# Attention scores in two visits a batch instead of five, with halves of 288 tokens, in a fused attention and mixture-of-experts kernel

## The chip, the cores and the metric

The kernel runs on one core of a Trainium2 chip, in one launch. The metric is the device time in microseconds (us) of that launch. Before the change the median of three timed runs is 524.84 us (524.31 to 526.43).

## The reference

Attention over 8 batches, 8 heads, 576 tokens and 64 values a head, with keys and values averaged over groups of 8 tokens (72 pooled keys); then a mixture of experts with 4 groups of 4 experts, one expert a token, on the 4608 x 512 result.

```
k_p = k.reshape(B, H, Sp, pool, D).mean(axis=3); v_p likewise     # pool = 8, Sp = 72
scores = scale * np.matmul(q, k_p.transpose(0, 1, 3, 2))
attn = np.exp(scores - scores.max(-1)); attn = attn / (attn.sum(-1) + 1e-09)
x = np.matmul(attn, v_p)              # -> (4608, 512) after joining the heads
g_idx = argmax(x @ w_group); g_w = softmax(x @ w_group)[g_idx]
e_idx = argmax(x @ w_expert[g_idx]);  e_w = softmax(...)[e_idx]
h = np.maximum(x @ w1[g, e], 0.0)     # 512 -> 1024
out = g_w * e_w * (h @ w2[g, e])      # 1024 -> 512
```

## The kernel before, in words

The work goes batch by batch (`b` = 0 to 7, 576 tokens each). While the experts' products of batch `b` run (class `Moe`, `m`), the attention of batch `b + 1` (`n`) is done between them, and the first steps of batch `b + 2` (`x`). Nearly all tokens of a batch choose one expert; its weights are loaded, and tokens with another expert are done behind the last batch (class `Left`).

The order is written out by hand in five plans, START, FIRST, SECOND, STEADY and LAST (lines 34 to 77): words such as `n.sc:1` or `m.up:3:0` are called one after the other by `run` (L880). START, FIRST and SECOND (batches 0 and 1) fix the order on all five engines. STEADY serves b = 2 to 6 and LAST b = 7; there the order is fixed on PE, DVE, POOL and SP, and ACT's is chosen by a scheduler. Every engine runs its instructions in its order.

The steps that matter here:

- `kr` (L252) folds 8 keys into one on DVE; `kt` (L282) transposes the pooled keys on PE into two `tp` banks: four transposes of 128 x 128 and, for the last 64 rows, one that reads partitions 64 to 127 alone (L286). ACT copies the result to `kT`. `qb` (L305) transposes the queries of a chunk on DVE into `qT`.
- `sc` (L310) is a **score visit**: the tokens of a batch lie in five chunks, `CH` (four of 128, one of 64), and one visit does a chunk. For each block of 32 tokens it issues 8 matmuls of 64 rows x 32 columns on parts of the PE array, into the two `sc` banks of PSUM. There is one pair of them (`ps_s`, L160), which the attention product `av` uses too.
- The softmax of a visit: `mx` (maximum, DVE, L329), `sb` (subtract on DVE, exponential on ACT, L335), `su_` (sum and reciprocal, DVE, L342), `nm` (scaling, POOL, L350), `pt` (transpose, DVE, L355).
- `av` (L363) multiplies the probabilities with the values for 256 or 320 tokens (`HALF`, L27), into the `sc` banks and two of the three `tp` banks. ACT takes the result, `avd` (L380) the low part on DVE. `rt` (L384), `route` and `main_expert` (L441) choose the experts; the count on PE (L437) is followed by the vote and by the weight loads on SP (L525).
- `load`, `cast` and `lo` bring a quarter of a weight matrix: DMA into one of 4 `sw` tiles, high part on ACT (L531), low part on POOL (L537). `split` is the last two.
- `up` (L543) does one of 8 blocks of 128 hidden values for one half: 12 matmuls over 256 or 320 tokens into one of three `mm` banks, then a ReLU on ACT (L556); `upd` (L558) takes the low part on DVE, and then the bank is free. `down` (L569) does a third of a chunk with 8 matmuls over 512 columns; after the third, ACT scales and stores. The last chunk of 64 tokens is L597 and is taken out by a copy on ACT (L602) and an add on DVE (L603).

One steady batch issues on PE: `up` of all blocks with four score visits between them, `av` twice, `rt` twice, 14 `down` with the routing, the key transposes and one score visit (the first of the batch after) between them.

Of the kernel before, what the change touches and what calls it, by code (L numbers as in the profile page):

```python
# [26 lines left out]
HALF = ((0, 256), (256, 320))  # L27
# [10 lines left out]
a.av:0:256 a.mx:2 a.sb:2 a.avd:0:256  # L38
# [20 lines left out]
m.load:2:3 m.up:1:1 m.upd:1:1 n.sc:2 n.mx:2 n.sb:2 n.qb:3 n.pt:1 x.load_k x.load_v
m.up:2:0 m.upd:2:0 n.su_:2 n.nm:2:p m.split:2:0 m.up:2:1 m.upd:2:1 m.up:3:0 m.upd:3:0 n.sc:3  # L60
n.mx:3 n.sb:3 n.qb:4 n.pt:2 m.up:3:1 m.upd:3:1 n.su_:3 n.nm:3:p m.split:2:1 m.up:4:0 m.upd:4:0 m.up:4:1 m.upd:4:1
n.sc:4 n.mx:4 n.sb:4 n.pt:3 m.up:5:0 m.upd:5:0 n.su_:4 n.nm:4:p m.split:2:2 m.up:5:1 m.upd:5:1 x.load_qb:0 x.load_qb:1
x.load_qb:2 x.load_qb:3 m.up:6:0 m.upd:6:0 m.split:2:3 m.up:7:0 m.upd:7:0 n.pt:4 n.av:0:256 n.avd:0:256 m.up:6:1 m.upd:6:1
m.up:7:1 m.upd:7:1 n.av:256:320 n.rt:0:256 n.avd:256:320
m.down:0 n.rt:256:320 x.kr:0 m.down:1 x.kr:1 m.down:2 n.route m.down:3 m.down:4 m.down:5 n.main_expert w.load:1:0 w.load:1:1 w.load:1:2 w.load:1:3
x.qb:0 n.gates n.gm_ n.keep_x m.down:6 x.vr:0 x.kt m.down:7 w.split:1:0 w.load:2:0 m.down:8 m.down:9
x.sc:0 x.mx:0 x.sb:0 x.qb:1 m.down:10 w.split:1:1 w.load:2:1 x.vr:1 x.vm m.down:11 x.su_:0 x.nm:0:p m.down:12 m.down:13
# [13 lines left out]
def attn_moe(ctx: ExitStack, tc: tile.TileContext, q, k, v, wg, we, w1, w2, out):  # L81
# [35 lines left out]
    probs = [keep.tile([128, 4, 160], F32, name=f"p{i}") for i in range(2)]  # L117
    for t in probs:
        nc.gpsimd.memset(t, 0.0)
    sums = [keep.tile([128, 4, 2, 2], F32, name=f"s{i}") for i in range(2)]  # L120
    for t in sums:
        nc.vector.memset(t, 1e-9)
# [57 lines left out]
    class Att:  # L180


        def __init__(s, b):
            s.b = b
            s.lt = s.v6 = s.pT = s.q = s.k = s.v = s.vf = None
            s.xt, s.qT, s.ss, s.su, s.ta, s.m = {}, {}, {}, {}, {}, {}

# [94 lines left out]
        def kt(s):  # L282
# [6 lines left out]
            nc.scalar.mul(out=s.kT[:, 512:576], in_=ps[1][:, 0:64], mul=0.015625)  # L289

        def qt(s, c):
# [10 lines left out]
            s.qT[c] = sm.tile([128, NG, 128], F32, name="qT")  # L302
            nc.scalar.copy(out=s.qT[c][:, :, 0:n], in_=ps.rearrange("p (g r) -> p g r", g=NG)[:, :, 0:n])

        def qb(s, c):  # L305
            o, n = CH[c]
            s.qT[c] = sm.tile([128, NG, 128], F32, name="qT")
            nc.vector.transpose(out=s.qT[c][:, :, 0:n], in_=s.q[:, 0:NG * S].rearrange("p (g t) -> p g t", g=NG)[:, :, o:o + n])

        def sc(s, c, where="s"):  # L310
            if where == "s":
                ps = ps_s.tile([128, 2, 512], F32, name="sc")
                s.ss[c] = [(slice(0, 2), ps)]
                ps = [ps[:, 0], ps[:, 1]]
            else:
                ps = [ps_m.tile([128, 512], F32, name="mm") for i in range(2)]
                s.ss[c] = [(slice(x, x + 1), ps[x].unsqueeze(1)) for x in range(2)]
            w = CH[c][1] // 32
            for t in range(w):
                for g in range(NG):  # L320
                    for x in range(2):
                        nc.tensor.matmul(ps[x][32 * g:32 * g + 32, SP * t:SP * t + SP], lhsT=s.qT[c][64 * x:64 * x + 64, g, 32 * t:32 * t + 32],  # L322
                                         rhs=s.kT[64 * x:64 * x + 64, SP * (2 * g + x):SP * (2 * g + x) + SP], start=(t == 0), stop=(t == w - 1))

        def views(s, c):
            w = CH[c][1] // 32
            return w, probs[(s.b * NC + c) % 2][:, 0:w, 0:2 * SP]

        def mx(s, c):  # L329
            w, p = s.views(c)  # L330
            m = s.m[c] = sm.tile([128, 2, 4], F32, name="mx")
            for x, ps in s.ss[c]:
                red(out=m[:, x, 0:w], in_=ps[:, :, 0:SP * w].rearrange("p x (t s) -> p x t s", s=SP), axis=AX.X, op=ALU.max)  # L333
# [594 lines left out]
```

## Time and profile before

| what | us |
|---|---|
| median of three timed runs | 524.84 |
| the profiled execution | 525.55 |
| its span, first to last instruction | 523.8 |
| PE busy in the span | 508.7 (97%) |
| DVE, POOL, ACT busy | 338.6, 257.1, 207.3 |

The profile is one execution. PE is TensorE with the matmuls, DVE VectorE, ACT ScalarE, POOL GpSimd, SP the queue that issues most DMAs. A row of a timeline merges equal instructions that follow one another: start, duration until the last has ended, engine, line, operation, `out<-in`, shape, count, and in brackets the idle time before it and what ended it. Matmuls overlap, so a row lasts a little beyond the start of the next; how long a stretch takes on PE is the distance between starts.

[...]

### The profile page before, as it was taken

Reading aid. Unit: us, or ns where it says so; the run is one execution under the profiler, and the core shown is the slowest. Engines: PE = TensorE matmul, PEld = TensorE weight load, DVE = VectorE, ACT = ScalarE, POOL = GpSimd, SP = SyncE. Lnnn points to the kernel's source line nnn. Section 1 sums busy time; section 2 is a strip of 40 time slices with the busy share of each in tenths; the row PEclk is TensorE's granted clock in tenths of the full one; section 3 lists DMA queues with packets and bytes.
Section 4 is the critical chain, followed back from the end, with each engine's and each line's share of the span. In section 5 each row is a group of like instructions: output and inputs, shape, how many; then the busy total and the mean of one; then the engine's idle time right before and its main releaser. Section 6 shows DMA issues by size and latency. Waiting matters only on the chain.

```text
span 523.8 us, 15045 instructions
## 1 busy us (share of the span) xinstructions
PE 508.7 (97%) x6061; PEld 446.4 (85%) x6061; DVE 338.6 (65%) x999; ACT 207.3 (40%) x394; POOL 257.1 (49%) x246
## 2 busy tenths in 40 slices
PE   8899989999989999999999999999999999999994
PEld 7698867898779988899889988899889988899873
DVE  6887878688366865397645956387646854287602
ACT  2444343453226531545235542455234541443211
POOL 2394866465536632867057741857049660511400
PEclk9999999999999999999999999999999999999998
DMA  8699398494256862749364771967555100835731
GB/s 284 182 261 197 85 257 229 73 241 103 52 173 181 236 99 79 244 148 186 73 199 155 211 119 45 332 229 201 91 169 185 63 1 21 268 125 195 231 139 36
DMA packets 118128, 83.75 MB, mean 160 GB/s; under 512 B 71034, under 2 KB 93818, under 8 KB 117800
## 3 DMA queue, kind: packets, MB, share of 16 engines
q1 hardware_dynamic: 113424, 75.70, 53.6%
q10 hardware_dynamic: 4600, 7.02, 3.8%
q8 instruction: 49, 0.80, 0.7%
q14 instruction: 23, 0.19, 0.1%
q0 software_dynamic: 32, 0.04, 0.0%
HBM read 77.31 MB, written 28.53 MB: 202 GB/s over the span
## 4 chain that ended last, share of the span: by engine, by line
PE 89%; DMA 4%; DVE 3%; POOL 1%; SPq 1%; issue 1%; ACT 1%; DVEq 0%; POOLq 0%
PE mm L554 34%; PE mm L580 32%; PE mm L597 5%; PE sc L322 5%; PE sc L373 4%; PE tp L390 3%; DMA vv<-in_v_dram 3%; DMA pT<-in_k_dram 1%; PE tp L285 1%; POOL vv L262 1%; PE tp L414 1%; PE tp L785 0%; PE tp L373 0%; PE tp L301 0%; PE tp L470 0%
## 5 line engine op out<-in xcount | busy, mean ns | idle before, releaser
L580 PE MATMUL mm<-w,ht 128*128 128x512 f32 x768 | 177.3, 383 | 0.0
L537 POOL TENSOR_TENSOR w<-sw,w 128x1024 fp32r<-128x1024 f32 (+2 forms) x87 | 148.7, 1731 | 40.3 <-ACT w L531 40.3
L580 PEld LDWEIGHTS mm<-w,ht 128*128 128x128 f32 x768 | 141.4, 189 | 21.6 <-issue 1.6
L554 PE MATMUL mm<-xb,w 128*128 128x320 f32 x768 | 115.9, 303 | 0.0
L554 PEld LDWEIGHTS mm<-xb,w 128*128 128x128 f32 x768 | 105.9, 189 | 4.3 <-issue 2.3
L554 PE MATMUL mm<-xa,w 128*128 128x256 f32 x768 | 96.3, 278 | 0.5 <-ACT xa L378 0.5
L554 PEld LDWEIGHTS mm<-xa,w 128*128 128x128 f32 x768 | 91.2, 191 | 3.5 <-ACT xa L378 1.0
L556 ACT ACTIVATE ht<-mm 128x320 fp32r<-128x320 f32 (+1 forms) x128 | 52.0, 408 | 81.3 <-PE mm L554 81.2
L353 POOL TENSOR_TENSOR p<-p,su 128x576 f32<-128x576 f32 (+1 forms) x40 | 42.2, 1057 | 71.5 <-DVE su L348 63.4
L531 ACT CAST w<-sw 128x1024 fp32r<-128x1024 f32 x64 | 66.0, 1041 | 20.5 <-DMA sw<-in_moe_w_dram 20.5
L566 DVE SCALAR_TENSOR_TENSOR ht<-mm,ht 128x160 fp32r<-128x160 f32 (+2 forms) x192 | 38.9, 258 | 18.2 <-ACT ht L556 17.7
L340 ACT ACTIVATE p<-p 128x576 f32<-128x576 f32 (+1 forms) x40 | 25.5, 637 | 54.5 <-DVE p L338 50.5
L491 POOL TENSOR_TENSOR mp<-oh,moh 128x80 f32<-128x80 f32 x8 | 3.4, 426 | 87.8 <-DVE moh L456 87.7
L591 ACT ACTIVATE y<-mm,gm 128x512 f32<-128x512 f32 x31 | 21.3, 686 | 52.3 <-PE mm L580 52.3
L333 DVE TENSOR_REDUCE mx<-sc 128x8 f32<-128x576 f32 (+1 forms) x38 | 26.1, 688 | 21.6 <-PE sc L322 21.6
L562 DVE SCALAR_TENSOR_TENSOR ht<-mm,ht 128x256 fp32r<-128x256 f32 x64 | 25.9, 406 | 14.3 <-ACT ht L556 14.0
L360 DVE STREAM_TRANSPOSE pT<-p 128x640 f32<-128x640 f32 (+1 forms) x40 | 30.5, 762 | 5.7 <-POOL p L353 5.7
L322 PE MATMUL sc<-kT,qT 64*32 64x72 f32 x2176 | 30.6, 229 | 2.0 <-DVE xa L382 1.6
L322 PEld LDWEIGHTS sc<-kT,qT 64*32 64x32 f32 x2176 | 23.9, 105 | 9.6 <-issue 7.0
L597 PE MATMUL mm<-w,ht 128*128 128x512 f32 x128 | 29.4, 381 | 0.0
L346 DVE TENSOR_REDUCE s<-p 128x8 f32<-128x576 f32 (+1 forms) x40 | 27.1, 677 | 1.2 <-ACT p L340 1.0
L338 DVE TENSOR_TENSOR p<-sc,mx 128x576 f32<-128x576 f32 (+1 forms) x38 | 26.4, 694 | 1.4
(212 smaller groups left out, 529.6 us busy)
## 6 DMA issues: line engine op xcount, KB each, us to landing
sw<-in_moe_w_dram SPq DMA_DIRECT2D x72, 512.0 KB
xscr<-xb SPq DMA_DIRECT2D x8, 1280.0 KB
vv<-in_v_dram SPq DMA_DIRECT2D x27, 320.0 KB
xscr<-xa SPq DMA_DIRECT2D x8, 1024.0 KB
q<-in_q_dram SPq DMA_DIRECT2D x112, 72.0 KB
kv<-in_k_dram SPq DMA_DIRECT2D x14, 512.0 KB
out_dram<-y ACTq DMA_DIRECT2D x23, 256.0 KB
pT<-xscr SPq DMA_DIRECT2D x4, 1152.0 KB
```

What stands on the lines that cost most here:

```text
L322: nc.tensor.matmul(ps[x][32 * g:32 * g + 32, SP * t:SP * t + SP], lhsT=s.qT[c][64 * x:64 * x + 64, g, 32 * t:32 * t + 32], rhs=s.kT[64 * x ...
L338: tt(out=p.rearrange("p t (x s) -> p x t s", x=2)[:, x], in0=ps[:, :, 0:SP * w].rearrange("p x (t s) -> p x t s", s=SP), in1=bc(s.m[c][:, ...
L346: red(out=two[:, :, :, 0], in_=p.rearrange("p t (x s) -> p t x s", x=2), axis=AX.X, op=ALU.add)
L353: (nc.vector if eng == "v" else nc.gpsimd).tensor_tensor(out=p, in0=p, in1=bc(s.su[c][:, 0:w], SP), op=ALU.mult)
L360: nc.vector.transpose(out=s.pT[:, :, o:o + n].rearrange("p j (t i) -> p t j i", i=32), in_=probs[(s.b * NC + c) % 2][:, 0:n // 32].rearran ...
L531: nc.scalar.copy(out=s.w[m, j][0], in_=raw)
L537: (nc.vector if eng == "v" else nc.gpsimd).tensor_tensor(out=wl[:, i:i + n], in0=s.raw[m, j][:, i:i + n], in1=wh[:, i:i + n].bitcast(F32), ...
L554: nc.tensor.matmul(ps[:, 0:n], lhsT=l[:, kc, fs], rhs=apart(s.a.xt[o][:, r, kc]), start=(kc == 0 and i == 0), stop=(kc == 3 and i == 2))
L556: nc.scalar.activation(out=halves(ht[:, sl]), in_=joined(ps[:, 0:n]), func=AF.Relu)
L566: stt(out=ht[:, at:at + hi - lo], in0=ps[:, a, lo:hi], scalar=0.0, in1=ht[:, t + lo:t + hi].bitcast(F32), op0=ALU.max, op1=ALU.subtract)
L580: nc.tensor.matmul(ps, lhsT=s.ht[f][:, 640 * l + o:640 * l + o + 128], rhs=apart(s.w[2, f // 2][r][:, f % 2, :]), start=(i == 0), stop=(i ...
L597: nc.tensor.matmul(ps, lhsT=s.ht[f][:, 512:640], rhs=apart(s.w[2, f // 2][r][:, f % 2, :]), start=(i == 0), stop=(i == 15))
```

## The change

From batch 3 on (`EARLY = 3`) the halves of attention and `up` are 288 and 288 tokens, and a half is also the chunk of a score visit: nine blocks of 32 tokens, two visits a batch. Seven blocks lie in the two `sc` banks, and two in two `tp` banks. The first visit's softmax goes in one step, the second's in a step A of four blocks and a step B of five. The exponential goes in pieces of at most five blocks. `probs` and `sums` become one tile each, `qT` one of 288 tokens. The key transposes take all 128 rows, for all batches. Batches 0 to 2 keep chunks and halves; in FIRST one `down` comes ahead of score visit 3 and a `pt` ahead of its maximum; in SECOND the second key fold and the transposes come ahead of `main_expert`. Of the plans' lines the diff shows only the parts that move.

```
-HALF = ((0, 256), (256, 320))
+EARLY = 3
+HALVES = (((0, 256), (256, 320)),) * EARLY + (((0, 288), (288, 288)),) * (B - EARLY)
+TW = 9
+STEPS = {"A": (0, 4), "B": (4, TW), "": (0, TW)}
 FIRST
-m.down:5 m.store:1 n.av:0:256 n.avd:0:256 n.sc:3 n.mx:3 n.sb:3 n.pt:2 m.down:6 n.su_:3 n.nm:3:p m.down:7 n.sc:4
+m.down:5 m.store:1 n.av:0 n.avd:0 n.pt:2 m.down:6 n.sc:3 n.mx:3 n.sb:3 m.down:7 n.su_:3 n.nm:3:p n.sc:4
 SECOND
-m.down:6 m.down:7 m.down:8 m.store:2 n.main_expert x.kr:1 w.load:1:0
+x.kr:1 m.down:6 m.down:7 x.qb:0 x.kt m.down:8 m.store:2 n.main_expert w.load:1:0
...
-            nc.tensor.transpose(out=ps[1][:, 0:64], in_=flat(s.kbt[64:128, 4]), identity=ident[64:128, 64:128])
+            nc.tensor.transpose(out=ps[1][:, 0:128], in_=flat(s.kbt[:, 4]), identity=ident)
...
+            if w > 7:
+                ps = [ps_t.tile([128, 512], F32, name="tp") for i in range(2)]
+                s.ss[c] += [(slice(x, x + 1), slice(7, w), ps[x].unsqueeze(1)) for x in range(2)]
+                banks.append(ps)
             for t in range(w):
+                bk, u = banks[t // 7], t % 7
...
+        def scored(s, c, step):
+            i, j, p, _ = s.views(c, step)
+            p = p.rearrange("p t (x s) -> p x t s", x=2)
+            for x, t, ps in s.ss[c]:
+                a, e = max(i, t.start), min(j, t.stop)
+                if a < e:
+                    ps = ps[:, :, SP * (a - t.start):SP * (e - t.start)].rearrange("p x (t s) -> p x t s", s=SP)
+                    yield ps, s.m[c][:, x, a:e], p[:, x, a - i:e - i]
...
+            for ps, m, p in s.scored(c, step):
+                red(out=m, in_=ps, axis=AX.X, op=ALU.max)
...
+            for a in range(0, j - i, 5):
+                z = min(a + 5, j - i)
+                nc.scalar.activation(out=p[:, a:z], in_=p[:, a:z], func=AF.Exp)
...
-            o, n = HALF[hf]
+            o, n = s.a.half[hf]
...
-            for a, lo, hi, at in ((0, 0, 160, 896), (1, 0, 96, 1056), (1, 96, 160, 576)):
-                t = o + 160 * a
+            m = n // 2
+            for a, lo, hi, at in ((0, 0, m, 640 + o), (1, 0, m - 64, 640 + o + m), (1, m - 64, m, 576)):
+                t = o + m * a
```

PE, at the start of the `up` products of a steady batch (L554 and L593 are `up`, L322 and L346 score visits). Before:

```order
L554 MATMUL mm<-xa,w 128x256 x12
L322 MATMUL sc<-kT,qT 32x72 x32
L554 MATMUL mm<-xb,w 128x320 x12
L554 MATMUL mm<-xa,w 128x256 x12
L554 MATMUL mm<-xb,w 128x320 x12
L322 MATMUL sc<-kT,qT 32x72 x32
L554 MATMUL mm<-xa,w 128x256 x12
L554 MATMUL mm<-xb,w 128x320 x12
L554 MATMUL mm<-xa,w 128x256 x12
L322 MATMUL sc<-kT,qT 32x72 x32
```

After:

```order
L593 MATMUL mm<-xa,w 128x288 x12
L593 MATMUL mm<-xb,w 128x288 x12
L346 MATMUL sc<-kT,qT 32x72 x56
L346 MATMUL tp<-kT,qT 32x72 x16
L593 MATMUL mm<-xa,w 128x288 x12
L593 MATMUL mm<-xb,w 128x288 x12
```

One visit of nine blocks stands behind the first pair, seven blocks into `sc` and two into `tp`; the other three visits of this stretch are gone.

PE in SECOND, around the key transposes (L285, L286; L302, L303) and the count for the vote (L437; L476); `mm<-w,ht` are `down` products. Before:

```order
L580 MATMUL mm<-w,ht 128x512 x24
L437 MATMUL tp<-oh,ones 128x80
L580 MATMUL mm<-w,ht 128x512 x8
L285 MATMUL tp<-ident,kb 128x128 x4
L286 MATMUL tp<-ident,kb 128x64
L580 MATMUL mm<-w,ht 128x512 x8
L322 MATMUL sc<-kT,qT 32x72 x32
```

After:

```order
L620 MATMUL mm<-w,ht 128x512 x16
L302 MATMUL tp<-ident,kb 128x128 x4
L303 MATMUL tp<-ident,kb 128x128
L620 MATMUL mm<-w,ht 128x512 x8
L476 MATMUL tp<-oh,ones 128x80
L620 MATMUL mm<-w,ht 128x512 x8
L346 MATMUL sc<-kT,qT 32x72 x56
L346 MATMUL tp<-kT,qT 32x72 x16
```

The transposes come two `down` earlier, ahead of the count, and the count one `down` and the transposes later; the visit behind has nine blocks.

ACT at the turn from one steady batch to the next (L531 and L570 are weight casts, L602 and L642 the copy of the last `down` block, L556 and L595 the ReLU of `up`). Before:

```order
L591 ACTIVATE y<-mm,gm 128x512
L531 CAST w<-sw 128x1024
L611 DMA out_dram<-y 128x512
L531 CAST w<-sw 128x1024
L602 COPY y<-mm 64x512
L556 ACTIVATE ht<-mm 128x256
```

After:

```order
L631 ACTIVATE y<-mm,gm 128x512
L570 CAST w<-sw 128x1024
L651 DMA out_dram<-y 128x512
L570 CAST w<-sw 128x1024 x3
L642 COPY y<-mm 64x512
L595 ACTIVATE ht<-mm 128x288
```

Two casts more, those of the first two quarters of the second weight matrix, stand ahead of the copy and of the first ReLU.

## Rows read from the trace of the kernel before

**Rows 1.** The page: busy time and share of each engine; the chain's shares.

```profile
PE 508.7 (97%) x6061; PEld 446.4 (85%) x6061; DVE 338.6 (65%) x999; ACT 207.3 (40%) x394; POOL 257.1 (49%) x246
...
PE 89%; DMA 4%; DVE 3%; POOL 1%; SPq 1%; issue 1%; ACT 1%; DVEq 0%; POOLq 0%
```

**Rows 2.** Timeline of PE, steady batch (b = 3): start, us, engine, line.

```profile
284.02 1.50 PE L554 MATMUL mm<-xa,w 128*128 128x256 f32 x12
285.35 1.80 PE L554 MATMUL mm<-xb,w 128*128 128x320 f32 x12
287.08 0.88 PE L322 MATMUL sc<-kT,qT 64*32 64x72 f32 x64
287.89 1.60 PE L554 MATMUL mm<-xa,w 128*128 128x256 f32 x12
289.33 1.80 PE L554 MATMUL mm<-xb,w 128*128 128x320 f32 x12
290.97 1.50 PE L554 MATMUL mm<-xa,w 128*128 128x256 f32 x12
292.40 0.89 PE L322 MATMUL sc<-kT,qT 64*32 64x72 f32 x64
...
298.01 0.48 PE L322 MATMUL sc<-kT,qT 64*32 64x72 f32 x32
```

**Rows 3.** Timeline of DVE, same batch: maximum of a visit.

```profile
288.19 0.75 DVE L333 TENSOR_REDUCE mx<-sc 128x8 f32<-128x576 f32 x1
...
299.12 0.45 DVE L333 TENSOR_REDUCE mx<-sc 128x4 f32<-128x288 f32 x1
```

**Rows 4.** Timeline of PE: key transposes (b = 3), full transposes in the last batch.

```profile
266.10 0.60 PE L285 MATMUL tp<-ident,kb 128*128 128x128 f32 x4
266.63 0.27 PE L286 MATMUL tp<-ident,kb 64*128 64x64 f32 x1
266.83 5.45 PE L580 MATMUL mm<-w,ht 128*128 128x512 f32 x24
...
487.10 1.09 PE L785 MATMUL tp<-ident,pT 128*128 128x128 f32 x8
487.95 1.97 PE L597 MATMUL mm<-w,ht 128*128 128x512 f32 x8
```

**Rows 5.** Timeline of PE in FIRST: score visit 3, second attention product.

```profile
76.54 0.87 PE L322 MATMUL sc<-kT,qT 64*32 64x72 f32 x64 [1.63 <-DVE xa L382]
...
85.93 0.50 PE L373 MATMUL sc<-pT,v 32*64 32x320 f32 x4
```

**Rows 6.** Timeline of DVE in FIRST: maximum of visit 3, last transpose.

```profile
77.45 0.76 DVE L333 TENSOR_REDUCE mx<-sc 128x8 f32<-128x576 f32 x1 [0.40 <-PE sc L322]
...
84.88 0.51 DVE L360 STREAM_TRANSPOSE pT<-p 128x320 f32<-128x320 f32 x1 [0.84 <-POOL p L353]
```

**Rows 7.** Timeline of PE in SECOND: `down` products, key transposes.

```profile
142.75 5.45 PE L580 MATMUL mm<-w,ht 128*128 128x512 f32 x24
...
149.98 0.38 PE L285 MATMUL tp<-ident,kb 128*128 128x128 f32 x2
151.83 0.44 PE L285 MATMUL tp<-ident,kb 128*128 128x128 f32 x2 [1.47 <-DVE kb L258]
```

**Rows 8.** Timeline of DVE in SECOND: routing's last operation, second key fold.

```profile
146.05 0.18 DVE L403 TENSOR_TENSOR o<-r,m 128x20 f32<-128x20 f32 x1
...
149.57 0.95 DVE L262 TENSOR_TENSOR kv<-kv 128x768 f32<-128x768 f32 x1
```

**Rows 9.** Timeline of ACT: end of SECOND, and the longest wait for weights.

```profile
160.40 1.06 ACT L531 CAST w<-sw 128x1024 fp32r<-128x1024 f32 x1 [0.37 <-DMA sw<-in_moe_w_dram]
161.48 0.58 ACT L602 COPY y<-mm 64x512 f32<-64x512 f32 x1
...
450.42 1.05 ACT L531 CAST w<-sw 128x1024 fp32r<-128x1024 f32 x1 [5.96 <-DMA sw<-in_moe_w_dram]
```

**Rows 10.** Busy time by stretch: span, engines, PEclk, DMA share, GB/s.

```profile
280.00:282.00 2.00, 2.00 (x65) 1.85 (x68) 0.69 (x2) 1.01 (x3) 2.00 (x3) 1.00 0.03 8
```

More of the change, by code (lines that the diff above doesn't have):

```diff
@@ L59 @@
[L59 to L67, printed above, removed]
+m.up:0:0 m.upd:0:0 m.split:1:2 m.load:2:2 n.pt:0:A m.up:0:1 m.upd:0:1 n.sc:1 n.mx:1:A m.up:1:0 m.upd:1:0 n.mx:1:B m.split:1:3
@@ L116, in attn_moe @@
     nc.vector.memset(hm[0:64, 4], 0.0)
[L117 to L122, printed above, removed]
+    probs = keep.tile([128, TW, 160], F32, name="p")
+    nc.gpsimd.memset(probs, 0.0)
+    sums = keep.tile([128, TW, 2, 2], F32, name="s")
+    nc.vector.memset(sums, 1e-9)
     desc4 = keep.tile([128, 4], F32, name="desc4")
@@ L321, in sc @@
                     for x in range(2):
[L322 to L333, printed above, removed]
@@ new lines, in mx, with sb @@
+        def mx(s, c, step=""):
+            if c not in s.m:
+                s.m[c] = sm.tile([128, 2, TW], F32, name="mx")
+            for ps, m, p in s.scored(c, step):
+                red(out=m, in_=ps, axis=AX.X, op=ALU.max)
+        def sb(s, c, step=""):
+            for ps, m, p in s.scored(c, step):
+                tt(out=p, in0=ps, in1=bc(m, SP), op=ALU.subtract)
+            i, j, p, _ = s.views(c, step)
+            for a in range(0, j - i, 5):
+                z = min(a + 5, j - i)
+                nc.scalar.activation(out=p[:, a:z], in_=p[:, a:z], func=AF.Exp)
@@ L346, in su_ @@
+        def su_(s, c, step=""):
+            i, j, p, two = s.views(c, step)
+            if c not in s.su:
+                s.su[c] = sm.tile([128, TW, 2], F32, name="su")
+            su = s.su[c][:, i:j]
             red(out=two[:, :, :, 0], in_=p.rearrange("p t (x s) -> p t x s", x=2), axis=AX.X, op=ALU.add)
@@ L374, in av, with avd, rt @@
                                          rhs=s.pT[32 * a:32 * a + 32, j, o:o + n], start=(i == 0), stop=(i == 2))
-            first = [(two[:, :, 0:n], slice(0, 2))] if o else [(two[:, i, 0:n], i) for i in range(2)]
-            s.ta[o] = first + [(one[i][:, 0:n], 2 + i) for i in range(2)]
-            for ps, g in s.ta[o]:
+            first = [(two[:, :, 0:n], slice(0, 2))] if h else [(two[:, i, 0:n], i) for i in range(2)]
+            s.ta[h] = first + [(one[i][:, 0:n], 2 + i) for i in range(2)]
+            for ps, g in s.ta[h]:
                 nc.scalar.mul(out=xt[:, 0, g], in_=ps, mul=0.125)
-        def avd(s, o, n):
-            for ps, g in s.ta[o]:
-                stt(out=s.xt[o][:, 1, g], in0=ps, scalar=0.125, in1=s.xt[o][:, 0, g].bitcast(F32), op0=ALU.mult, op1=ALU.subtract)
-        def rt(s, o, n):
+        def avd(s, h):
+            for ps, g in s.ta[h]:
+                stt(out=s.xt[h][:, 1, g], in0=ps, scalar=0.125, in1=s.xt[h][:, 0, g].bitcast(F32), op0=ALU.mult, op1=ALU.subtract)
+        def rt(s, h):
             if s.lt is None:
                 s.lt = sm.tile([128, S], F32, name="lt", bufs=1)
+            o, n = s.half[h]
             sl = slice(o, o + n)
@@ L507, in keep_x @@
             left = nc.sync.value_load(s.lf[0:1, 0:1], min_val=0, max_val=1)
-            for o, n in HALF:
-                nc.sync.dma_start(out=xscr[s.b][:, :, :, o:o + n], in_=s.xt[o].bitcast(F32), cond=left, cond_hint=False)
+            for h, (o, n) in enumerate(s.half):
+                nc.sync.dma_start(out=xscr[s.b][:, :, :, o:o + n], in_=s.xt[h].bitcast(F32), cond=left, cond_hint=False)
     class Moe:
```

109 lines of the change are left out of this document (65 added, 44 removed).

## The prediction

> **What bounds the kernel now.** I read the page first. PE is busy for 97% of the span, and the chain that ended last runs through PE for 89% of it; DMA has 4%, DVE 3%, ACT and POOL 1% each [rows 1]. So time is won only where PE stops doing something, or stops waiting. Next I read PE's timeline through one steady batch (the plan STEADY with b = 3), start to start: the matmuls of `up`, `down` and `sc` follow one another without any idle time in the brackets [rows 2]. The work of the softmax on DVE, POOL and ACT is covered there. Then I looked for PE's few waits: one for DVE ahead of a score visit in FIRST [rows 5] and one for DVE inside the key transposes in SECOND [rows 7]. The rest of the gain or loss must come from how long PE needs for the same matrix work, and from new waits.
>
> The profiled execution took 525.55 us, 1.75 more than its span of 523.8, and 0.71 more than the median of the three timed runs, 524.84. The sum is made against 525.55 and then moved by 0.71.
>
> **Score visits, 25 to 10.** Batches 3 to 7 have five visits each before and two after; the number of score matmuls is the same (18 blocks of tokens a batch). A visit of 4 blocks shows 0.88 us and one of 2 blocks 0.48 [rows 2], so the body goes by blocks, 0.20 us each, and is not saved. What is saved are the edges. An `up` of 256 tokens takes 1.33 us from its start to the next start when another `up` follows (284.02 to 285.35), 1.43 ahead of a visit (290.97 to 292.40) and 1.44 behind one (287.89 to 289.33). For 320 tokens it is 1.64 without a visit (289.33 to 290.97) and 1.73 ahead of one (285.35 to 287.08). So a visit costs 0.10 on each side, 0.20 together. 15 visits fewer at 0.20: **-3.0**. Bounds: the 0.08 that is left of 0.88 when four blocks at 0.20 are taken off may be per visit too (0.28, -4.2); or the step inside a nine-block visit from the `sc` banks to the `tp` banks costs an edge of 0.10 again, ten times (-2.0). I take the middle one, which rests on the most rows.
>
> **Halves of 288.** A pair takes 1.33 + 1.64 = 2.97 now, and twice the value between, 1.485, is 2.97 again. Attention and routing go by columns in the same way: **0** (a bound of 0.02 a pair in either direction would be 0.8 over 40 pairs).
>
> **Softmax in steps.** A DVE step over 576 elements takes 0.75 us and one over 288 takes 0.45 [rows 3], so about 0.15 is fixed. The five-block step becomes three pieces for the maximum and three for the subtraction, about 1.15 us each. In the up stretch PE needs 2.97 us a pair; in it DVE has two `upd` (four pieces with 576 elements together: 4 x 0.15 + 0.60 = 1.20) and at most one four-block and one five-block step (0.75 + 1.15), 3.10 in all, and only some of the eight pairs have both. Before, a single visit brought maximum, subtraction, transpose and query transpose between two `upd`. What grows is the down stretch, where one nine-block visit replaces a four-block one. With three `mm` banks PE may run ahead of DVE by an `up` and more: **0** here; the cover is that lead of some 1.4 us, against an excess of 0.13, and if a step were late by more, PE would pay the rest in each batch.
>
> **Full key transposes.** Four transposes of 128 columns and one of 64 take 0.73 us, from 266.10 to 266.83, and the last alone 0.20; eight full ones in the last batch take 0.85, 0.106 each [rows 4]. Five at 0.106 are 0.53 (-0.20); five at the pace of these four, 0.133, are 0.67 (-0.07); the old last one plus 64 more columns would be +0.07. I take -0.1, nearest to the two rows of full transposes, eight times: **-0.8**, bounds -1.6 and +0.5. [...]
>
> **FIRST: one `down` moved ahead of score visit 3.** PE waits 1.63 us at 76.54, because `avd` on DVE still reads the `sc` banks [rows 5]. Now `m.down:6` (about 1.8 us) stands there, and that wait goes. What is late next is `n.av:1` at 85.93, which needs the whole softmax of this batch. PE would come to it 1.63 earlier, at 84.3. But its last input, the transpose at 84.88, ends 0.5 ahead of it and hangs on a DVE chain that begins with the maximum at 77.45, which waited only 0.40 for PE [rows 6]. The plan now puts the transpose of visit 2 (about 0.8) ahead of that maximum, and it starts near 77.8. I follow the chain to a transpose at about 85.1 and `n.av:1` at 85.65, 0.3 earlier: **-0.3**, and a new wait of PE of about 1.4 there. Bounds -1.6 and +0.5.
>
> **SECOND: key fold and transposes ahead of the vote on the expert.** Now PE stands in the key transposes from 149.98 to 151.83, 1.85 us, for the second fold, which runs from 149.57 [rows 7, 8] and so needs 2.26 until PE goes on. In the new order PE reaches the transposes after two of the three `down` that start at 142.75 (two thirds of 5.45: at 146.4). DVE is not free for the fold before the routing's last operation at 146.05; from 146.25 it needs its 2.26, to 148.5. So PE stands about 2.1 instead of 1.85: **+0.3**; bounds -1.7 (no wait at all) and +1.0. The count for the vote comes behind the transposes (0.6) and one `down` (1.8), near 150.9 and not near 148.2, and with it batch 2's first weight loads, 2.7 us late. ACT already waits for the fourth of them before the cast at 160.40, and behind that cast stand the copy of the last `down` block and the first ReLU [rows 9]. At 163.1 they are still just in time, since the nine-block visit now lies between; but little is left: **+0.2**, bounds 0 and +1.5.
>
> **Sum.** -3.0 - 0.8 - 0.3 + 0.3 + 0.2 = -3.6. 525.55 - 3.6 = 521.95; less 0.71 it is **521.2 us**. Its own range, by the bounds that are likeliest to meet, is 519.5 to 523.
>
> **Rivals.**
> *The early stages and the tail eat it.* FIRST +0.5, SECOND +1.0, the late weights +1.5, transposes 0, visits -2.5: +0.5, so up to 525.3, and 524 with half of that. For it: SECOND moves a wait and does not remove it. Against it: the five steady stretches don't depend on it.
> *Slower: ACT's casts.* From batch 3 on, four casts of weights in a row (order below) now stand ahead of the copy that frees a `mm` bank and of the first ReLU. If the second load of w2 isn't there, ACT blocks. Each cast takes 1.06 and the copy 0.58 [rows 9]; with a DVE add of at most 0.75 that is about 2.6 us to the bank's release, and PE needs it two `up` and a nine-block visit later, 2 x 1.49 + 2.0 = 5.0: it decides from about 2.4 us of lateness on. One cast in this trace waited 5.96 for its load [rows 9]. At 4.4 us late PE loses 2 in each of four batches, +8.0: 529.3. Against it: the DMA engines are nearly idle from 280 us on (share 0.03), when both loads have been issued [rows 10], and the cast is wanted near 281.4.
> *The early waits go altogether.* -1.6 in FIRST and -1.7 in SECOND with the steady -3.8: -7.1, 517.7. Against it: both chains above.
>
> **How the numbers follow.** Forecast 0.61, early stages eat it 0.20, casts 0.11, early waits gone 0.08. About 0.5% (2.6 us: under 522.2 or over 527.5) is what can be told from no change. Three quarters of the forecast and all of the last rival lie under 522.2: 0.54 faster. A quarter of the forecast and nearly all of the first rival: 0.33 the same. The casts and a little of the first rival: 0.13 slower. The range, 518.0 to 525.6, holds the forecast and most of the two milder rivals and leaves out the casts.
>
> **What would show it.** In the profile after: two score visits a batch near 1.9 us each with PE busy on both sides; pairs of `up` at 2.97; key transposes near 0.63 instead of 0.73; a PE wait near 1.4 us at the second attention product of FIRST and near 2 us in the key transposes of SECOND; and no wait of ACT for a load ahead of the copy in steady batches. The forecast is wrong if a nine-block visit takes more than 2.1 us, if PE waits anywhere in a steady batch, or if the edges of a visit don't shrink with their number.

## The result, and the profile after

The changed kernel takes 529.57 us (median of 14 runs, 527.01 to 532.23); the kernel before, in the runs beside it, 525.31 (524.31 to 527.56). The ratio is 1.0074, with a 95% interval of 1.0056 to 1.0091: slower by 4.3 us, where 521.2 was forecast. The profiled execution took 530.5 us with a span of 528.8, and the mean granted clock of PE is 0.985 of full instead of 0.997.

The waits of PE come first (engine, line and what it waited for: us in total, times, longest):

```profile
PE mm L593 <- DVE y L643: 3.8, 1, 3.8
PE tp L346 <- issue: 3.6, 1, 3.6
PE tp L302 <- DVE kb L275: 2.6, 2, 1.7
...
PE sc L411 <- DVE pT L397: 1.2, 1, 1.2
```

The 1.7 and the 1.2 are the waits forecast for SECOND and FIRST (the other wait on L302 is in START). The first two lines stand in steady batches, where the forecast had none; each comes once. In rows of the changed kernel L302 and L303 are the key transposes, L346 `sc`, L593 `up`, L620 and L637 `down`, L570 the casts, L642 and L643 the copy and the add of the last chunk, L564 the weight loads and L548 the stores of x.

A batch is measured from the first `up` to that of the next. Before, b = 2 to 5 took 59.80 to 59.81 us each and b = 6 58.26. After, the starts are 162.05, 220.63, 285.52, 343.88, 407.78 and 464.32: 58.58, **64.89**, 58.36, **63.90** and 56.54 us for b = 2 to 6. So three of the five steady batches became 1.2 to 1.7 shorter, and two lost 6.5 and 5.5 against 58.36. The rest of the difference of the two profiles (+5.0): START +2.0, FIRST -0.55, SECOND +0.19, what follows b = 6 -1.41.

**The stop inside a visit, b = 3.** PE's timeline at the place that answers to [rows 4], and into b = 4, which answers to [rows 2]:

```profile
264.50 0.60 PE L302 MATMUL tp<-ident,kb 128*128 128x128 f32 x4
264.94 0.27 PE L303 MATMUL tp<-ident,kb 128*128 128x128 f32 x1
264.97 1.97 PE L620 MATMUL mm<-w,ht 128*128 128x512 f32 x8
266.87 1.34 PE L346 MATMUL sc<-kT,qT 64*32 64x72 f32 x107
...
268.06 0.34 PE L346 MATMUL tp<-kT,qT 64*32 64x72 f32 x13
272.01 0.49 PE L346 MATMUL tp<-kT,qT 64*32 64x72 f32 x15 [3.61 <-issue]
272.44 9.79 PE L620 MATMUL mm<-w,ht 128*128 128x512 f32 x32
282.06 3.62 PE L637 MATMUL mm<-w,ht 128*128 128x512 f32 x16
285.52 1.63 PE L593 MATMUL mm<-xa,w 128*128 128x288 f32 x12
286.99 1.63 PE L593 MATMUL mm<-xb,w 128*128 128x288 f32 x12
288.55 1.34 PE L346 MATMUL sc<-kT,qT 64*32 64x72 f32 x107
...
290.23 1.74 PE L593 MATMUL mm<-xa,w 128*128 128x288 f32 x12
```

PE stops for 3.61 us ahead of the last 15 of the visit's 144 matmuls (two for each product), and waits for no engine: "issue". The same 32 `down` matmuls behind the visit take 9.62 us here (272.44 to 282.06) and 7.02 in b = 2. Busy time by stretch shows why (columns: window, span, busy time of PE, of its weight loads, of DVE, ACT and POOL, then granted clock, DMA share and GB/s):

```profile
268.00:270.00 2.00, 0.41 (x40) 0.25 (x27) 1.21 (x1) 1.04 (x1) 0.33 (x1) 1.00 1.00 327
270.00:272.00 2.00, 0.00 (x0) 0.00 (x0) 0.00 (x0) 1.04 (x1) 2.00 (x2) 0.73 1.04 347
272.00:274.00 2.00, 1.99 (x19) 1.51 (x19) 1.42 (x3) 0.00 (x0) 2.00 (x2) 0.50 0.68 137
274.00:276.00 2.00, 2.00 (x6) 1.56 (x5) 1.93 (x4) 0.00 (x0) 2.00 (x2) 0.50 0.77 251
```

While PE stood, the granted clock fell to 0.50 of full, and it is still 0.50 from 274 to 276, under `down`: 2.6 us on top of 3.61. The DMA engines were full (w1 loads issued at 264.91). One more queue moved in that stop: of the DMA view from 269 to 270 us (packets, MB, share of 16 engines):

```profile
q1 hardware_dynamic: 263, 0.25, 84.3%
q8 instruction: 1, 0.02, 6.1%
```

The queue "instruction" moved 49 packets in the run, 0.80 MB. Counting shows what they bring. The trace has 12239 instructions of PE: 6061 matmuls, as many weight loads, and 117 of its sequencer, the part that waits and branches. Taken in order of time, PE stops here after 7105 of them, which is 193 + 27 x 256, and the packet that starts at 269.54 us is the 27th. All 17 issue waits of PE of 0.2 us or more in the profiles of these runs (ten of the fourteen profiles have one or more) stand after 193 + 256 x k instructions, where k is the number of packets so far, and each ends 2.2 to 3.0 us after the start of the k-th packet. So the queue brought PE's program in pieces of 256 instructions, and PE stood when the next piece wasn't there.

A visit of nine blocks has 288 instructions, more than a piece. At b = 3 it begins three instructions ahead of a piece, so that the whole piece lies inside it: PE used it up in 1.30 us (266.88 to 268.18). The packet with the next piece started 2.66 us after PE had begun on this one, while the DMA engines were full. The visit that starts at 410.81 us (b = 6) holds a whole piece too, and PE doesn't stop in it: there the DMA engines are idle, and the packet started at 410.17, before PE began on the piece.

```profile
410.00:412.00 2.00, 2.00 (x124) 1.85 (x126) 2.00 (x6) 1.12 (x3) 2.00 (x2) 1.00 0.04 12
```

So the long stop took both: a piece that is used up within one visit, and full DMA engines.

Of the 48 ends of pieces in this profile, this is the only one with an issue wait of 0.1 us or more, and it cost 3.61.

**The casts, start of b = 5.** SP, ACT and PE, one fence each:

```profile
333.00 0.60 SPq L548 DMA_DIRECT2D xscr<-xa  x1
333.91 2.40 SPq L548 DMA_DIRECT2D xscr<-xb  x1
336.94 11.63 SPq L564 DMA_DIRECT2D sw<-in_moe_w_dram  x3
```

```profile
341.28 1.05 ACT L570 CAST w<-sw 128x1024 fp32r<-128x1024 f32 x1
...
342.23 1.04 ACT L570 CAST w<-sw 128x1024 fp32r<-128x1024 f32 x1
348.74 1.05 ACT L570 CAST w<-sw 128x1024 fp32r<-128x1024 f32 x1 [5.47 <-DMA sw<-in_moe_w_dram]
350.04 1.04 ACT L570 CAST w<-sw 128x1024 fp32r<-128x1024 f32 x1 [0.25 <-DMA sw<-in_moe_w_dram]
351.11 0.58 ACT L642 COPY y<-mm 64x512 f32<-64x512 f32 x1
351.71 0.41 ACT L595 ACTIVATE ht<-mm 128x288 fp32r<-128x288 f32 x1
```

```profile
346.92 1.34 PE L346 MATMUL sc<-kT,qT 64*32 64x72 f32 x107
...
352.46 2.90 PE L593 MATMUL mm<-xa,w 128*128 128x288 f32 x12 [3.81 <-DVE y L643]
355.15 2.19 PE L593 MATMUL mm<-xb,w 128*128 128x288 f32 x12
357.17 1.63 PE L593 MATMUL mm<-xa,w 128*128 128x288 f32 x12
```

In this batch some tokens choose a second expert, so the stores of x to DRAM (2.3 MB) are really made; in the other batches they are skipped (the issue of one at 268.71 us takes 0.14 and not 0.60). The w2 loads share the DMA engines with them, the cast waits 5.47, and behind it stand the copy, DVE's add and the bank that PE needs. The stretch that answers to [rows 10], just ahead of the landing, has a DMA share of 1.03 and not 0.03:

```profile
346.00:348.00 2.00, 2.00 (x115) 1.85 (x115) 0.00 (x0) 0.00 (x0) 2.00 (x1) 1.00 1.03 393
```

Behind PE's wait the granted clock is 0.50:

```profile
354.00:356.00 2.00, 2.00 (x10) 2.00 (x10) 0.91 (x3) 0.41 (x1) 0.00 (x0) 0.50 1.03 382
```

The next two `up` take 2.69 and 2.02 us instead of 1.47 each, 1.77 more. With the wait that is 3.81 + 1.77 = 5.6.

**START.** The 2.0 us are not the change's: in a second profile of each kernel (e11, e12 below) the changed kernel is the earlier one.

### The profile page after: what moved, and what is told of

The parts are those of the page before. It is cut to its first block, busy times and chain, and to the rows that moved or that the text cites. A ratio compares the mean times of both kernels' runs of the same rounds, so it can differ in the third digit from the quotient of the medians.

```text
span 528.8 us, 14968 instructions
## 1 busy us (share of the span) xinstructions
PE 506.4 (96%) x6061; PEld 448.1 (85%) x6061; DVE 332.3 (63%) x968; ACT 207.4 (39%) x389; POOL 255.9 (48%) x235
## 3 DMA queue, kind: packets, MB, share of 16 engines
q10 hardware_dynamic: 4600, 7.02, 3.8%
## 4 chain that ended last, share of the span: by engine, by line
PE 83%; DMA 7%; DVE 4%; issue 2%; ACT 1%; SPq 1%; POOL 1%; DVEq 0%; ACTq 0%; POOLq 0%
PE mm L593 35%; PE mm L620 28%; PE mm L637 5%; PE sc L411 4%; PE sc L346 3%; DMA vv<-in_v_dram 3%; PE tp L429 3%; DMA sw<-in_moe_w_dram 3%; DMA q<-in_q_dram 1%; PE tp L346 1%; PE mm L914 1%; PE tp L453 1%; POOL w L576 1%; PE tp L411 0%; PE tp L825 0%
## 5 line engine op out<-in xcount | busy, mean ns | idle before, releaser
L620 PE MATMUL mm<-w,ht 128*128 128x512 f32 x768 | 180.2, 388 | 0.0
L620 PEld LDWEIGHTS mm<-w,ht 128*128 128x128 f32 x768 | 143.1, 191 | 22.5 <-issue 1.8
L593 PE MATMUL mm<-xb,w 128*128 128x288 f32 (+1 forms) x768 | 108.8, 294 | 0.0
L593 PE MATMUL mm<-xa,w 128*128 128x288 f32 (+1 forms) x768 | 102.0, 286 | 4.4 <-DVE y L643 3.8
L593 PEld LDWEIGHTS mm<-xb,w 128*128 128x128 f32 x768 | 101.4, 190 | 3.2 <-issue 2.2
L593 PEld LDWEIGHTS mm<-xa,w 128*128 128x128 f32 x768 | 96.3, 192 | 6.9 <-DVE y L643 4.0
L595 ACT ACTIVATE ht<-mm 128x288 fp32r<-128x288 f32 (+2 forms) x128 | 52.0, 410 | 88.5 <-PE mm L593 86.3
L570 ACT CAST w<-sw 128x1024 fp32r<-128x1024 f32 x64 | 65.7, 1043 | 32.3 <-DMA sw<-in_moe_w_dram 32.1
L389 POOL TENSOR_TENSOR p<-p,su 128x576 f32<-128x576 f32 (+3 forms) x30 | 40.4, 1347 | 73.5 <-DVE su L384 69.1
L606 DVE SCALAR_TENSOR_TENSOR ht<-mm,ht 128x64 fp32r<-128x64 f32 (+4 forms) x192 | 38.0, 253 | 17.1 <-ACT ht L595 16.2
L601 DVE SCALAR_TENSOR_TENSOR ht<-mm,ht 128x288 fp32r<-128x288 f32 (+1 forms) x64 | 27.5, 431 | 21.4 <-ACT ht L595 20.9
L397 DVE STREAM_TRANSPOSE pT<-p 128x640 f32<-128x640 f32 (+2 forms) x35 | 29.9, 854 | 6.2 <-POOL p L389 6.2
L643 DVE TENSOR_TENSOR y<-mm,y 64x512 f32<-64x512 f32 x8 | 5.5, 682 | 40.3 <-ACT y L642 40.3
L382 DVE TENSOR_REDUCE s<-p 128x8 f32<-128x576 f32 (+3 forms) x30 | 25.8, 861 | 6.0 <-ACT p L375 6.0
L637 PE MATMUL mm<-w,ht 128*128 128x512 f32 x128 | 29.4, 381 | 0.0
L411 PE MATMUL sc<-pT,v 32*64 32x288 f32 (+2 forms) x384 | 26.9, 409 | 1.2 <-DVE pT L397 1.2
L411 PE MATMUL tp<-pT,v 32*64 32x288 f32 (+2 forms) x384 | 26.9, 409 | 0.0
L637 PEld LDWEIGHTS mm<-w,ht 128*128 128x128 f32 x128 | 24.0, 189 | 3.5 <-issue 0.2
```

Of the source, the lines that this page charges most:

```text
L382: red(out=two[:, :, :, 0], in_=p.rearrange("p t (x s) -> p t x s", x=2), axis=AX.X, op=ALU.add)
L389: (nc.vector if eng == "v" else nc.gpsimd).tensor_tensor(out=p, in0=p, in1=bc(s.su[c][:, i:j], SP), op=ALU.mult)
L397: nc.vector.transpose(out=s.pT[:, :, o + 32 * i:o + 32 * j].rearrange("p j (t i) -> p t j i", i=32), in_=probs[:, z + i:z + j].rearrange(" ...
L411: nc.tensor.matmul(banks[a][64 * x:64 * x + 64, 0:n], lhsT=s.v6[32 * a:32 * a + 32, 5 if x and i == 0 else j, :], rhs=s.pT[32 * a:32 * a + ...
L570: nc.scalar.copy(out=s.w[m, j][0], in_=raw)
L593: nc.tensor.matmul(ps[:, 0:n], lhsT=l[:, kc, fs], rhs=apart(s.a.xt[hf][:, r, kc]), start=(kc == 0 and i == 0), stop=(kc == 3 and i == 2))
```

## The experiments

The intervals are ratios to the kernel before. A "batch" is again `up` to `up`. Diffs of a plan show the words of STEADY that move (in e6 those of START).

**e1, ACT by the plan.**

```
-            with tc.manual_schedule(engines=MANUAL[1]):
+            with tc.manual_schedule(engines=MANUAL[b == B - 1]):
```

> The changed kernel with ACT's order in STEADY taken from the plan too, so that the copy that frees a mm bank and the first ReLUs come ahead of the casts of w2 (before: behind four casts in a row). Theory A (the order of the casts is the cause of the wait at 352 us): the PE wait of 3.81 for the add at the start of b = 5 and the stretch at the lower clock behind it go; that batch took 64.1 us from up to up against 58.4 to 58.6 of undisturbed ones, so -5.5: about 524 us. Rival B (the loads are late whatever ACT does): PE then waits for w2 later, in the first down of that batch, and the time stays at 528 to 530. The other disturbed batch, b = 3 with 64.9 us, is left as it is by both.

Measured: 531.07 us, ratio 1.0081 (1.0057 to 1.0106). The wait for the casts went: b = 5 takes 59.79 us like b = 4. But each steady up stretch took about 31.4 us instead of 30.0, five times +1.4. ReLUs now stand behind exponentials that wait for DVE (1.25 us at 299.50), and PE waits for the `ht` of five of them, 4.0 us in all; the rest of the 7 isn't traced. Theory A is right on the cause; the time I expected was wrong, since the plan's order has a price of its own. The stop in the visit came again, ahead of the same 15 matmuls:

```profile
274.67 0.49 PE L346 MATMUL tp<-kT,qT 64*32 64x72 f32 x15 [3.56 <-issue]
```

**e2, first visit two `down` later.**

```
-x.sc:0 x.mx:0 m.down:8 x.sb:0 m.down:9 x.qb:1 m.down:10
+m.down:8 m.down:9 x.sc:0 x.mx:0 m.down:10 x.sb:0 x.qb:1
```

> The changed kernel with the first nine-block visit of a batch (sc:0 of the batch after next) moved two down later in STEADY, to the place where the kernel before had it (behind down:9), when the w1 loads have landed. Theory A: PE stood 3.61 us inside the visit at 268 us because the next piece of its own program came late through DMA engines that were full (share 1.00 to 1.04 from 266 to 272); at the later place the share is 0.7 to 0.8 and the stall goes, with the lower clock behind it: batch b = 3 back from 64.9 to 58.6, so -6.3, 523 to 524 us. Rival B: such a stall is chance and belongs to no place; then the time stays at 529 to 530 and the profile shows an issue wait of 2 us or more inside some other visit. The wait at 352 us for the casts stays in both.

Measured: **521.27 us**, 0.9893 (0.9862 to 0.9923). There is no stop in a visit, and b = 3 takes 58.35 us; a short issue wait, 0.49, stands in a `down` of b = 4. One thing was not as I expected: the DMA engines are full at the new place too.

```profile
270.00:272.00 2.00, 2.00 (x147) 1.60 (x145) 0.18 (x1) 1.24 (x2) 2.00 (x1) 1.00 1.00 337
```

Two things differ. The two `down` (32 instructions) now take up part of the piece that lay inside the visit, and PE needs 4.47 us for it instead of 1.30. And the next piece, the 27th packet, came from 263 to 264 us, ahead of the loads, when that packet was all that the DMA engines moved. The DMA view of that stretch:

```profile
q8 instruction: 1, 0.02, 7.2%
```

So the visit had what it needed. Why the packet didn't come then in the changed kernel too isn't settled. In none of the profiles does one start with more than 298 PE instructions left to run. At 263.6 us the changed kernel had 293 left, as here, and its DMA engines were idle (share 0.00 from 262 to 264). What the trace has there: a wait of the visit for DVE's queries, just ahead of the piece, ends on PE's sequencer at 266.03, and the w1 packets begin at 265.97. That this kept the packet back is a guess, which no run tests.

The wait for the casts was there, but only 1.89 us long; that the time lies below the 523 to 524 of theory A is mostly this. Why it was shorter isn't traced.

**e3, both edits.**

> Both edits of the two kernels above at once (ACT by the plan, first visit two down later). If both theories A hold, the two disturbed batches come back to 58.6 us: 529.6 - 5.5 - 6.3 = about 518 us, and the mean granted clock comes back to 0.997. If only one holds, 523 to 524. If neither, 529.

Measured: 542.25 us, 1.0288 (1.0254 to 1.0322): a clear miss. With the visit later and ACT by the plan, POOL's scaling of the first visit comes late; DVE's transpose waits for it ahead of `upd`, PE for `upd` (2.7 at the longest), and the clock falls again (0.59 from 234 to 238 us). Two issue waits stand in this profile too, 0.55 and 1.09, the longer one in the visit of b = 6 that holds a whole piece.

```profile
232.22 0.84 DVE L397 STREAM_TRANSPOSE pT<-p 128x640 f32<-128x640 f32 x1 [6.00 <-POOL p L389]
```

**e4, stores of x behind the w2 loads.**

```
-x.qb:0 n.gates n.gm_ n.keep_x m.down:6
+x.qb:0 n.gates n.gm_ m.down:6
...
-w.split:1:1 w.load:2:1 x.vr:1
+w.split:1:1 w.load:2:1 n.keep_x x.vr:1
```

> The changed kernel with the stores of x to DRAM (keep_x, 2.3 MB, done only in batches with tokens of a second expert) moved in STEADY behind the second load of w2, so that the weight loads go first; ACT's order is that of the changed kernel. Theory A (these stores make the w2 loads late in the one steady batch that has them, at 333 to 348 us): the cast of w2 no longer waits 5.47, the PE wait of 3.81 goes, about 524 us. Rival B (the loads are late by their own amount): 529 to 530, and the cast still waits 4 us or more.

Measured: 522.76 us, 0.9935 (0.9908 to 0.9963). PE's wait at the start of b = 5 is gone, so the stores ahead of the loads were what made them late. The stop in the visit stays, at the same instruction:

```profile
270.88 0.36 PE L346 MATMUL tp<-kT,qT 64*32 64x72 f32 x15 [3.88 <-issue]
```

**e5, e2 and e4 together.**

> The two edits that helped, together: first nine-block visit two down later, stores of x behind the second w2 load, ACT's order left to the scheduler. If they take away two separate disturbances (the stall inside the visit, batch b = 3, about 6 us; the late casts, batch b = 4, 3.6 to 5.5 us), the times add up: the profile of the kernel with the late visit has one batch of 33.6 us in the up stretch against 30.0 of the others, so 521.3 - 3.6 = 517.7; the kernel with the late stores has one down stretch of 34.1 against 28.4, so 522.8 - 5.7 = 517.1. Rival: the two were one disturbance seen twice (a PE that stood once meets the loads at another time), then 521.

Measured: **518.03 us**, 0.985 (0.9835 to 0.9865), 7.6 faster than the kernel before and the best version here. All of b = 3 to 6 are undisturbed: 58.35, 58.34, 58.34 and 56.25. The time lies within 1 us of both sums and 3 under the rival's 521, so the two disturbances were separate. (Measured from the changed kernel, e2 alone gained 8.3, e4 alone 6.8 and both 11.5: e2 had already taken half of the wait for the casts with it.) PE in b = 3 and 4:

```profile
265.61 0.60 PE L302 MATMUL tp<-ident,kb 128*128 128x128 f32 x4
266.05 0.27 PE L303 MATMUL tp<-ident,kb 128*128 128x128 f32 x1
266.07 5.43 PE L620 MATMUL mm<-w,ht 128*128 128x512 f32 x24
271.43 1.34 PE L346 MATMUL sc<-kT,qT 64*32 64x72 f32 x108
...
273.09 3.72 PE L620 MATMUL mm<-w,ht 128*128 128x512 f32 x16
276.64 3.62 PE L637 MATMUL mm<-w,ht 128*128 128x512 f32 x16
280.10 1.63 PE L593 MATMUL mm<-xa,w 128*128 128x288 f32 x12
281.57 1.63 PE L593 MATMUL mm<-xb,w 128*128 128x288 f32 x12
283.13 1.35 PE L346 MATMUL sc<-kT,qT 64*32 64x72 f32 x108
```

**e6, PE's program shifted.** A function `tiny` issues `z` matmuls of 8 columns into an `mm` bank.

```
-t.warm:10 t.turn_wr
+t.warm:10 t.tiny:32 t.turn_wr
```

> The changed kernel with 32 tiny matmuls of 8 columns more at the start, so that every later instruction of PE lies further on in its program; nothing else moves. Theory A (PE's program comes in pieces by DMA, and the visit at b = 3 used up a piece while the DMA engines were full): the place of the stall hangs on where the pieces end, so the issue wait of 3.6 us inside that visit goes or moves into another visit or another place of it (it stood ahead of the last 15 of the matmuls into tp in each profile so far). Rival B (the stall belongs to that visit's data or banks, whatever the program's pieces): the same 3.6 us ahead of the same 15 matmuls. The start costs 1 to 3 us.

Measured: 542.9 us in one run. The start cost more than I expected (first `up` at 36.1 instead of 27.5). The visit of b = 3 ran without a stop, and a stop stood in another visit (start of b = 2), ahead of the last 5 matmuls:

```profile
178.26 0.49 PE L346 MATMUL tp<-kT,qT 64*32 64x72 f32 x23
181.17 0.32 PE L346 MATMUL tp<-kT,qT 64*32 64x72 f32 x5 [2.42 <-issue]
```

The DMA share from 178 to 180 us is 0.98. Issue waits of 0.8 to 1.8 stood at five other places too. One run that also moves everything by 8.6 us could be chance, but the count settles it: all six waits stand after 193 + 256 x k instructions (this one after 4801, k = 18), and of this kernel's visits of nine blocks the one with the stop is the only one that holds a whole piece. The visit of b = 3, behind 64 instructions more, no longer does. So the place hangs on where the pieces of the program end, as theory A says; rival B falls.

**e7, first visit ahead of the loads.** `qb:0` goes behind the second key fold, `kt` behind `down:3`, the visit behind the count.

```
-x.kr:1 m.down:2 n.route m.down:3 m.down:4 m.down:5 n.main_expert w.load:1:0
+x.kr:1 m.down:2 x.qb:0 n.route m.down:3 x.kt m.down:4 m.down:5 n.main_expert x.sc:0 w.load:1:0
```

> The changed kernel with the first nine-block visit moved ahead, straight behind the count of the vote, before the w1 loads are issued; key transposes and the first query transpose go ahead with it. Theory A (full DMA engines while a visit uses PE's program up fast): the DMA engines are idle there (share 0.00 at 262 to 264 us), so no issue wait inside the visit, and batch b = 3 comes back to about 58.5 us; the wait for the casts at b = 5 stays: 523 to 524 us. Rival B (a visit of nine blocks uses PE's program up faster than it can come, whatever else the DMA does): an issue wait of 1 us or more in the visit of some batch, and 527 to 530.

Measured: 523.02 us, 0.9952 (0.9938 to 0.9967), as theory A expected. No visit has an issue wait; the wait for the casts stayed, 3.1 us, and b = 3 took 58.84. A short rest of the stop is left in the `down` right behind the visit, after 7105 instructions again:

```profile
262.00:264.00 2.00, 2.00 (x113) 1.84 (x116) 0.87 (x5) 0.69 (x1) 0.00 (x0) 1.00 0.03 8
...
265.40 1.89 PE L620 MATMUL mm<-w,ht 128*128 128x512 f32 x8 [0.38 <-issue]
```

Here the visit holds nearly the whole piece (PE used it up in 1.64 us), but the packet started 0.07 us after PE had begun on it, and not 2.66. So with idle DMA engines 0.38 us of the stop is left, and the 2.6 us by which the packet started later are the greater part of the 3.61.

**e8, the kernel before with full key transposes alone.** Line 286 takes all 128 rows, and line 289 copies columns 64 to 127.

> The kernel before with the full key transposes alone. The trace after shows 0.47 us for the five (264.50 to 264.97) against 0.73 in the kernel before, 0.26 each, eight times: -2.1 us against the kernel before if the transposes' whole gain reaches the end; -0.8 by the forecast; 0 if PE waits for the same DVE and DMA results anyway.

Measured: 524.11 us, 0.9965 (0.9949 to 0.998). That is -1.8 by the ratio, with an interval of -2.7 to -1.1, so of the three expectations only -2.1 lies in it. A steady batch takes 59.52 instead of 59.81.

**e9, e5 with whole softmax steps.** The steps A and B of `mx`, `sb`, `su_`, `nm` and `pt` become one each, at the place of A (`pt:1` at B).

> The kernel of e5 (518.0 us) with the second visit's softmax in whole steps of nine blocks in place of steps of four and five: DVE then has steps of some 1.2 to 2 us between two upd. Theory A (PE's lead of an up and more over DVE covers such a step, as the forecast assumed for the steps): 518, up stretches of 30.0 us as before. Rival B (PE waits for the mm bank each time DVE is that late): the up stretch grows by 0.3 to 1 us in each of four batches, 519 to 522, and waits of up for DVE ht show.

Measured: 518.72 us, 0.9855 (0.9833 to 0.9876), which can't be told from e5. DVE's transpose is then one step of 1.68 us, and PE's one wait for DVE's `ht` is 0.2 us. The steps cost and win nothing that can be seen.

**e10, the kernel before with the late stores alone.**

> The kernel before with the stores of x behind the second w2 load, nothing else: a control for e5. Theory A (in the kernel before these stores disturb nothing, since no cast stands ahead of the copy of the last block, and no PE wait shows there): the time of the kernel before, 525 to 526. Rival B (part of what e5 won belongs to the late stores and not to the change): 522 to 524.

Measured: 525.65 us, 0.9993 (0.9978 to 1.0008): nothing. (Two casts do stand ahead of the copy of the last block in the kernel before, but they are of w1, and in the steady batches of its first profile they waited for no load.) What e5 wins over the kernel before is the change's, once its two disturbances are out.

**e11 and e12, both kernels once more.**

> The kernel before once more, for a second profile of its START: if the wait for qT near 20 us and the time of the first up (25.5 us in its first profile, 25.2 to 27.5 in those of the other kernels, whose START is nearly the same) change from run to run, the 2.0 us that the changed kernel's profile lost in START are not the change's. If they are the change's, first up at 25.5 again.

> The changed kernel once more. Theory A (both disturbances have a fixed place in the program and the data): the issue wait ahead of the last 15 matmuls into tp in the visit at b = 3, 3.5 to 3.9 us, and the wait for the casts at b = 5, 2 to 4 us, both come again, 528 to 532. Rival B (chance): one or both are missing, or stand in another batch. First up at 25.2 to 27.5.

Measured: 526.54 and 529.38 us. First `up` at 27.24 in the kernel before and at 25.04 in the changed one, the other way round than in the first pair; so START's 2.0 us are not the change's. PE in START of the kernel before, run again:

```profile
20.56 1.13 PE L322 MATMUL mm<-kT,qT 64*32 64x72 f32 x64 [1.97 <-ACT qT L303]
...
22.23 3.05 PE L874 MATMUL mm<-ones 128*128 128x256 f32 x8
```

After the wait of 1.97 the same eight matmuls took 3.05 at a granted clock of 0.50; in e12, without that wait, 1.99. The two disturbances of the changed kernel came again, 3.48 (ahead of the same 15) and 3.8.

## Why the prediction was wrong

**The terms of the sum were right in sign or near nothing, and the steady ones too small.**
- *Score visits, -3.0.* The edges are as forecast: an `up` takes 1.56 ahead of a visit and 1.57 behind it, against 1.47, so 0.19 a visit (e2 and e5, b = 4). But I took it that the body isn't saved. A nine-block visit takes 1.67 and not 9 x 0.20, as blocks are a little cheaper in a long run: 3.34 a batch for 18 blocks instead of 0.81 x 4 + 0.41 = 3.65 (start to next start, as 287.08 to 287.89 in [rows 2]). Edges -0.6 and body -0.3 make -0.9 a batch, five times -4.5, a little beyond the bound of -4.2.
- *Halves, 0.* A pair takes 2.94 and not 2.97, which is -0.24 a batch, or -1.2 over the 40 pairs, beyond the bound of 0.8.
- *Key transposes, -0.8.* Five take 0.46 instead of 0.73 (e5), so -0.27 each time, eight times -2.2; e8 gave -1.8 by itself. Of the estimates there, five at the pace of the eight full ones (-0.20 each, -1.6 in all) came nearest; the old last one plus 64 more columns (+0.5) had the wrong sign. e8 shows the gain; why the transpose over 64 rows cost more isn't shown.
- *Softmax in steps, 0.* This was right: e9 with whole steps takes the same time.
- *FIRST -0.3, SECOND +0.5 with the late weights.* They came to -0.55 and +0.19 with the key transposes' -0.27 in each, so to -0.28 and +0.46 without. Both waits came where they were expected: 1.2 for 1.4, and 2.05 (147.18 to 149.23) for 2.1.

-0.9, -0.24 and -0.27 are -1.4 a batch; e5's 59.81 to 58.35 is -1.46. The forecast had -0.7.

**The step that failed is that nothing new in a steady batch makes PE wait.** The sum has no term for it, and the prediction names such a wait as a sign of being wrong. It failed at two places:
- *A cost that I didn't see.* In the step on the visits I counted blocks, edges and banks. I didn't count that the first visit moved forward by two `down`, into the stretch in which the w1 loads fill the DMA engines, nor that PE's own program comes through these engines. It cost 6.5 us in one batch. The 1% of "issue" in the page's chain [rows 1] was no sign of it: in the trace before it is 3.2 us in bits of 0.17 at most, and PE's longest issue wait is 0.11.
- *A rival taken too low.* "Slower: ACT's casts" had the right place and chain, and a chance of 0.11. The argument against it rests on rows of b = 3 [rows 10], where the stores of x are skipped. The trace before had the batch that makes them too. At the same place one batch on, its DMA share is 1.06 and not 0.03:

```profile
340.00:342.00 2.00, 2.00 (x77) 1.86 (x75) 0.89 (x2) 1.20 (x3) 2.00 (x2) 1.00 1.06 398
```

The rival cost 5.5 in one batch, not 2 in each of four. Its price left out what the clock takes after PE has stood (1.77). It also counted one cast behind the late load where two stood: from the late cast's start (348.74) to PE's going on (352.46) it is 3.7 us and not 2.6 (and its terms, 1.06, 0.58 and 0.75, add up to 2.4).

In the profile the two disturbances are +12.1 together. The rest is -9.1 (the five batches -7.3, FIRST and SECOND -0.4, what follows b = 6 -1.4, of which e8 shows 1.0 with nothing changed there), and START is +2.0: +5.0. That the two disturbances are what turned the gain into a loss is shown by e5, which takes both away and lands at 518.0, 3.2 under the forecast. That PE's program is behind the "issue" wait is shown by the count, 256 instructions to a piece at every one of the 17 waits, by the stop's moving with e6, and by its fixed instruction in four profiles (the first, e1, e4, e12). That full DMA engines make the short stop a long one is shown by e7 (0.38 us, share 0.03 at the packet's start, against 3.61 at 1.00 to 1.04) and by the visit of b = 6 in the changed kernel (no stop, share 0.04); why the packet wasn't under way before the engines filled stays open (e2).

## What to carry to other kernels

Before work is put into longer runs of small matmuls, count their instructions against the pieces in which the program arrives (256 instructions here), and keep a run that holds a whole piece out of stretches in which the DMA engines are full (a share of 0.98 to 1.04 where such a visit stood here). An "issue" wait that returns at the same instruction is a sign of this (here the same 15 matmuls in four profiles); count the instructions ahead of it to be sure. A cover read from one batch holds only for the batches with the same transfers, so look for the one with conditional stores and read the same row there. And price a long PE wait with the lower clock behind it: here, at 0.50, 2.6 and 1.8 us on top of waits of 3.61 and 3.81.

## What was not expected of the hardware

- PE can stand for want of its own program. It stood for 3.61 us at a DMA share of 1.00 to 1.04 (the changed kernel, b = 3) and for 2.42 at 0.98 (e6), in visits that issue 288 instructions in 1.7 us, and for 0.38 us where the share was 0.03 when the packet started (e7, 262 to 264 us).
- PE's program came in pieces of 256 instructions. In these profiles a packet started with at most 298 instructions left to run, and where PE stood it went on 2.2 to 3.0 us after the packet's start.
- A long visit was denser than short ones: 0.186 us a block in nine (e5), 0.203 in four [rows 2].
- The last key transpose, over 64 rows, cost more than one over 128: five take 0.46 us when all are full (e5), and 0.73 with it [rows 4].
